# Token weights between the attention pairs, token products in thirds: the first batch of an attention and mixer kernel

## The chip, the cores and the metric

The kernel runs on one core of a Trainium2 chip. The metric is the device time of one execution in microseconds, as a median over runs. The core has five engines that run side by side and meet through semaphores: TensorE (PE in the profile; PEld is its weight load), VectorE (DVE), ScalarE (ACT), GpSimd (POOL) and SyncE (SP), which here issues nearly all DMAs. SBUF is the on-chip working memory, PSUM the eight banks into which matrix products go.

## The reference

There are 4 batches, 8 heads, 768 positions and head width 64. For each head, attention sees a band of 31 neighbours and 24 block summaries. A block is 32 positions: its key is the maximum over the block, its value the mean.

```
k_sum = k.reshape(B, H, nb, block, D).max(axis=3)
v_sum = v.reshape(B, H, nb, block, D).mean(axis=3)
scores_l = scale * q @ k^T          (kept where |i - j| < 16)
scores_s = scale * q @ k_sum^T + log(32)
a = softmax(concat(scores_l, scores_s));  x = a @ concat(v, v_sum)
```

The heads are laid side by side (x: 4 x 768 x 512), and a mixer follows: a token part that mixes positions through 256 columns, then a channel part through 1536 columns.

```
h = relu(x^T @ w_tok1) @ w_tok2;   u = x + h^T
out = u + relu(u @ w_ch1) @ w_ch2
```

## The kernel before, in words

**Stages.** The heads of a batch are taken in 4 pairs (`p`), each in two halves of the positions (`g`). For a pair, `key_blocks` reduces the block maxima (`ks`) and copies them behind the 96 window columns of each of the 12 key tiles (`k[:, :, 96:]`), PE makes the scores (`sc`), DVE adds the mask and finds the row minimum of the negated scores (`lowest`, one custom instruction for each of 128 x 120 scores, with a second one that reads out `den`), ACT takes the exponential (`power`), PE turns the result (`et`), ACT copies it out (`eT`), PE multiplies by the values (`av`), and DVE divides and writes `x` (`rec`, `x`). The channel part then runs one step behind: `ch1` makes `hp` from `u` and `w1`, ACT and DVE split it into high and low part `h`, and `ch2` adds to the four `acc` banks with `w2`. While it runs on one batch, the attention of the next is woven in. So only the first batch's attention stands alone: it fills the first part of the span.

**The first batch.** Its value means come from PE (`vm`, in `first_means`): 24 products for a pair, the two heads written to partitions 64 to 87 and 96 to 119 of one bank. Two DVE copies take them to `vs`, and two POOL copies spread them into the value tiles (`v`). `tok1` makes the first token product `t1p` of a pair: 12 products of 128 x 128 (each shows as two records in the trace), 6 position tiles times 2 column halves, bound to all three parts of `wt1`. ACT (`Relu`) and DVE split it into `t1`. `tok2` makes `up` from `x`, `t1` and both halves of the second token matrix, `wt2`, which it needs whole.

**Weights.** The weights are 64-bit words. `w_tick(i)` loads two jobs of 256 KB into a staging tile and turns them into 32-bit numbers: two ACT passes (`absolute` into `wt` or `wb`, `last_bits` into `wp`), one POOL pass (`clamp`), two DVE passes (`shift` into `wp`, `sign` into `wt` or `wb`). Ticks 0 to 2 fill the three parts of `wt1` directly. From tick 3 on there follow two ACT copies (high part) and two POOL subtractions (low part): ticks 3 to 5 are `wt2`, then each channel weight tile takes one tick. `WTAGS` says whose memory the staging tile of a tick borrows; a tick's load waits until that slot is free.

**What sets the order.** Each piece of work is an `add(engine, time, function, reads, writes, rank)`. `Plan` plays the list through with these times; of what is ready on an engine it takes the lowest rank, and among equals the earliest written. The order that comes out is then fixed: every engine works strictly in it, so a step whose input is late holds all behind it. The ranks are `R_H, R_EVAC, R_ATT, R_LATER, R_W, R_BACK`, lowest first. `bank(name, tags)` goes round the PSUM banks named in `tags`; `att` and `mm` have two banks each, `acc0` to `acc3` one. `APART` puts a pad of so many 32-bit words in front of the first tile of a tag in SBUF, so it shifts addresses and nothing else.

**Lines.** Numbers are of the kernel before: `key_blocks` L347 (maximum) and L356 (copy); `first_means` L376 (PE), L396 (DVE copies), L383 (POOL); `tok1` L752; `split_t1` L733 and L738; `tok2` L832, L840, L879, L884; `w_tick` L1473 and L1479 (ACT), L1486 (POOL), L1491 and L1498 (DVE), L1518 (ACT), L1524 (POOL); `lowest` L478, `power` L488; warm-up L1537. `between` on DVE, which the change calls, is one instruction with two tensor inputs:

```
nc.vector.scalar_tensor_tensor(
    out=out_, in0=left, scalar=1.0, in1=right, op0=ALU.mult, op1=op
)
```

Of the kernel before, what the change touches and what calls it, by code (L numbers as in the profile page):

```python
# [202 lines left out]
def tile_attention_mixer(  # L203
# [74 lines left out]
    def tok_bank(name, first=False):  # L278
        if state["phase"] == "start":
            return bank(name, ["acc0", "acc1"] if first else ["att", "att", "acc2"])  # L280
        return bank(name, BANKS[state["phase"]])
# [58 lines left out]
    def key_blocks(p):  # L340

        if p >= B * NP:
            return
        kt, ks = k_t[p], sbuf([P, NB], "ks", f"ks_{p}", 2)
        add(
            "dve", 0.98,
            lambda: nc.vector.tensor_reduce(  # L347
                out=ks.t.rearrange("p (t r) -> p t r", r=2),
                in_=kt.t[:, :, 16 : 16 + QT].rearrange("p t (r c) -> p t r c", c=32),
                axis=AX, op=ALU.max,  # L350
            ),
            reads=[(kt, 0)], writes=[(ks, 0)], rank=R_ATT,
        )
        add(
            "dve", 0.33,
            lambda: nc.vector.tensor_copy(  # L356
                kt.t[:, :, WIN:], ks.t.unsqueeze(1).broadcast_to([P, NT, NB])
            ),
            reads=[(ks, 0)], writes=[(kt, 1)], rank=R_ATT,
        )  # L360
# [4 lines left out]
    def first_means(p):  # L365

        pt, cs = vm_bank, slice(DTOK + D * p, DTOK + D * (p + 1))
        s = sbuf([P, 2 * D], "vs", f"vs_0_{p}", 2)
# [4 lines left out]
        def sums():  # L373
            for t in range(NT):
                for j in range(2):
                    nc.tensor.matmul(  # L376
                        pt.t[at[j] : at[j] + NB, cs],
                        lhsT=means[:, NB - 2 - 2 * t : 2 * NB - 2 - 2 * t],
# [3 lines left out]
        def spread(n, j):  # L382
            nc.gpsimd.tensor_copy(  # L383
                v_t[n].t[WIN:NC, :, :D],
                s.t[WIN:NC, j * D : (j + 1) * D].unsqueeze(1).broadcast_to([NB, NT, D]),
# [5 lines left out]
        )  # L391
        for j in range(2):
            n = 2 * p + j
            add(
                "dve", 0.15,
                lambda j=j: nc.vector.tensor_copy(  # L396
                    s.t[WIN:NC, j * D : (j + 1) * D], pt.t[at[j] : at[j] + NB, cs]
                ),
                reads=[(pt, p)], writes=[(s, j)], rank=R_EVAC,
            )  # L400
            add(
                "pool", 0.95, lambda n=n, j=j: spread(n, j), reads=[(s, j)],
                writes=[(v_t[n], 1)], rank=R_ATT,
            )
# [340 lines left out]
    def tok1(b, p):  # L745
# [3 lines left out]
        def products():  # L749
            for k in range(DTOK // P):  # L750
                for T in range(TT):
# [3 lines left out]
                        start=(T == 0), stop=(T == TT - 1),  # L755
                    )

        add(
            "pe", 2.8, products, reads=x_keys(b, p) + [(wt1, i) for i in range(3)],
            writes=[(pt, 0)], rank=R_ATT,  # L760
        )
# [629 lines left out]
    APART = {"u1": 32, "u0": 16, "ot": 32, "t1": 32, "w1": 16}  # L1391
# [32 lines left out]
    WTAGS = ["u0"] * 6 + ["k", "k", "q", "v", "x", "x"] * 4  # L1424
    assert 2 * len(WTAGS) == len(jobs)

    def w_tick(i, behind=()):
# [21 lines left out]
        first, rank = two[0][2] is None, R_ATT if i < 3 else R_LATER if i < 6 else R_W  # L1449
# [10 lines left out]
        else:  # L1460
            pb = bank(f"wp_{i}", ["acc3"] if i < 10 else ["att"])
# [45 lines left out]
        add("dve", 0.7, shift, reads=parts, writes=[(pb, 0)], rank=rank)  # L1507
        add("dve", 0.7 if room else 0.85, sign, reads=[*keys, (pb, 0)], writes=parts, rank=rank)
# [23 lines left out]
    add("dve", 0.3, lambda: nc.vector.memset(warm.t, 0.0), writes=[(warm, 0)])  # L1532
    pw = mm_bank("warm")

    def warm_up():
        for _ in range(17):
            nc.tensor.matmul(pw.t, lhsT=warm.t[:, :P], rhs=warm.t, start=True, stop=True)  # L1537

    add("pe", 5.2, warm_up, reads=[(warm, 0)], writes=[(pw, 0)])
# [170 lines left out]
```

## Time and profile before

| what | value |
|---|---|
| median of 3 runs | 562.3 us (561.27 to 563.73) |
| the profiled execution | 563.8 us, span 561.4 us |
| PE busy | 546.0 us, 97% of the span |
| PE weight loads | 484.5 us, 86% |
| DVE, ACT, POOL busy | 337.7, 267.9, 265.7 us |
| mean DMA rate | 179 GB/s |
| PE's share of the chain that ended last | 84% |

The span is the time between the first and the last instruction of the profiled execution; the execution's own time is 2.4 us longer. Busy times are sums over instructions, and PE's are modelled, because products overlap. The timeline lists instructions in order of time; the chain of waits goes back from the last instruction to whatever released each step; a waits row gives the total, the count and the longest wait. The start of the profile, up to the first `hp` at 63 us, is where nearly everything of the change lies.

### The profile page before, as it was taken

To read this page: it belongs to the slowest core of one execution; us is meant where nothing else is said; L and a number is where in the kernel's file an instruction comes from. 1 tells how busy PE (TensorE), PEld (TensorE's weight loads), DVE (VectorE), ACT (ScalarE), POOL (GpSimd) and SP (SyncE) were. 2 spreads that over 40 slices of the span, in tenths; PEclk is the share of its full clock that TensorE was granted. 3 is DMA by queue.
4 is the path that set the end of the run, shared out by engine and by line. 5 is a ranking of instruction groups with operands and counts; after the bars stand their busy time and mean duration, and the time that the engine had idled before them with its cause. 6 is when DMAs were issued, how large, how long until landed. Compare 5 with 4: busy or idle time off the path is not lost.

```text
span 561.4 us, 12755 instructions
## 1 busy us (share of the span) xinstructions
PE 546.0 (97%) x4625; PEld 484.5 (86%) x4625; DVE 337.7 (60%) x949; ACT 267.9 (48%) x771; POOL 265.7 (47%) x344
## 2 busy tenths in 40 slices
PE   7979999999989999999999999999999999999997
PEld 4769888878889988888799997888789999999997
DVE  4985668866553346455463436444352584898974
ACT  4776788853674334222252215332234342567642
POOL 2555478832134320168997420059879612454111
PEclk9979999999999999999999999999999999999999
DMA  8952569674655018759695506768788664543531
GB/s 330 396 177 76 188 196 281 184 234 140 193 171 164 19 43 213 207 175 255 200 279 147 110 18 187 168 173 232 184 239 260 175 231 133 179 139 109 177 103 63
DMA packets 134030, 100.30 MB, mean 179 GB/s; under 512 B 88272, under 2 KB 112464, under 8 KB 133968
## 3 DMA queue, kind: packets, MB, share of 16 engines
q1 hardware_dynamic: 133824, 99.31, 59.1%
q8 instruction: 36, 0.59, 0.4%
q14 instruction: 26, 0.21, 0.1%
q10 hardware_dynamic: 144, 0.20, 0.1%
HBM read 69.39 MB, written 28.31 MB: 174 GB/s over the span
## 4 chain that ended last, share of the span: by engine, by line
PE 84%; DMA 7%; DVE 4%; SPq 1%; ACT 1%; issue 1%; POOL 1%; ACTq 0%; DVEq 0%; POOLq 0%
PE hp L901 25%; PE acc L944 25%; PE up L840 6%; PE t1q L799 5%; PE av L598 3%; PE pb L1174 3%; PE sc L464 3%; PE t1p L752 2%; PE pa L1174 2%; PE qb L1174 2%; PE qc L1174 2%; PE pc L1174 2%; DMA vb<-in_vb 1%; DMA k<-in_kw 1%; PE et L528 1%; PE qa L1174 1%
## 5 line engine op out<-in xcount | busy, mean ns | idle before, releaser
L944 PE MATMUL acc<-h,w 128*128 128x512 f32 (+1 forms) x864 | 162.3, 337 | 0.0
L901 PE MATMUL hp<-u,w 128*128 128x512 f32 (+1 forms) x864 | 161.6, 336 | 0.0
L901 PEld LDWEIGHTS hp<-u,w 128*128 128x128 f32 x864 | 133.1, 188 | 18.2 <-issue 1.4
L944 PEld LDWEIGHTS acc<-h,w 128*128 128x128 f32 x864 | 132.0, 188 | 18.2 <-ACT h L913 1.4
L488 ACT ACTIVATE e<-e,den 128x120 f32<-128x120 f32 x192 | 69.8, 385 | 58.6 <-DVE den L478 52.7
L913 ACT ACTIVATE h<-hp 128x512 fp32r<-128x512 f32 (+1 forms) x72 | 35.2, 488 | 117.0 <-PE hp L901 116.6
L918 DVE SCALAR_TENSOR_TENSOR h<-hp,h 128x512 fp32r<-128x512 f32 (+1 forms) x72 | 39.7, 552 | 74.3 <-ACT h L913 74.1
L1021 POOL TENSOR_TENSOR s<-s,w 128x256 f32<-128x256 f32 x84 | 62.0, 744 | 5.1
L983 POOL TENSOR_TENSOR ot<-ot,u 128x512 f32<-128x512 f32 (+1 forms) x24 | 23.7, 1015 | 59.5 <-DVE ot L975 27.7
L478 DVE CUSTOM_DVE_ANT_0 e<-sc,mask_sb 128x120 f32<-128x120 f32 x192 | 41.3, 277 | 15.0 <-PE sc L464 12.3
L1524 POOL TENSOR_TENSOR w<-wb,w 128x256 fp32r<-128x256 f32 x48 | 34.6, 742 | 9.4 <-ACT w L1518 9.2
L840 PE MATMUL up<-wt,t 128*128 128x512 f32 (+2 forms) x192 | 39.0, 343 | 0.0
L447 POOL MEMSET e<- 128x48 f32 x16 | 2.2, 138 | 67.9 <-DMA away<-e 33.3
L785 POOL TENSOR_TENSOR xs<-x,xs 128x512 fp32r<-128x512 f32 x18 | 23.2, 1291 | 21.1 <-ACT xs L780 21.1
L840 PEld LDWEIGHTS up<-wt,t 128*128 128x128 f32 x192 | 30.4, 189 | 2.4
L420 DVE TENSOR_REDUCE vs<-vb 96x8 f32<-96x256 f32 (+1 forms) x40 | 18.4, 461 | 17.1 <-DMA vb<-in_vb 17.0
L464 PEld LDWEIGHTS sc<-k,q 64*64 64x64 f32 x768 | 19.9, 132 | 10.0 <-issue 9.2
L799 PE MATMUL t1q<-xs,ws 128*128 128x256 f32 x216 | 28.4, 283 | 0.0
L464 PE MATMUL sc<-k,q 64*64 64x120 f32 x768 | 26.8, 271 | 1.5 <-DVE k L356 1.5
L799 PEld LDWEIGHTS t1q<-xs,ws 128*128 128x128 f32 x216 | 27.0, 190 | 0.3
L488 ACT ACTIVATION_READ_ACCUMULATOR e<-e,den 128x1 f32 x144 | 27.1, 188 | 0.0
L598 PEld LDWEIGHTS av<-v,eT 120*64 120x64 f32 x768 | 23.8, 138 | 3.8 <-issue 2.4
(128 smaller groups left out, 870.5 us busy)
## 6 DMA issues: line engine op xcount, KB each, us to landing
w<-in_w_ch SPq DMA_DIRECT2D x48, 256.0 KB
k<-in_kw SPq DMA_DIRECT2D x16, 720.0 KB
v<-in_vw SPq DMA_DIRECT2D x24, 288.0 KB
q<-in_q SPq DMA_DIRECT2D x16, 384.0 KB
away<-e SPq DMA_DIRECT2D x16, 384.0 KB
eT<-away SPq DMA_DIRECT2D x64, 96.0 KB
sums<-s SPq DMA_DIRECT2D x24, 256.0 KB
w2d<-w SPq DMA_DIRECT2D x12, 512.0 KB
```

Of the source, the lines that this page charges most:

```text
L464: nc.tensor.matmul(tiles[j].t[c * QT : (c + 1) * QT, i * NC : (i + 1) * NC], lhsT=qt.t[rows, t * QT : (t + 1) * QT], rhs=kt.t[rows, t, :], ...
L478: nc.vector.tensor_tensor_reduce(out=e.t[:, j, i * P : i * P + NC], in0=tiles[j].t[:, i * NC : (i + 1) * NC], in1=mask_sb[:, mv, :], op0=A ...
L488: nc.scalar.activation(ei, ei, AF.Exp, bias=den_t[n].t[:, 1, T : T + 1], scale=-1.0, accum_out=den_t[n].t[:, 0, T : T + 1] if p >= NP else ...
L598: nc.tensor.matmul(pv[cs, T], lhsT=eT[:NC, T % (TT // 2), cs], rhs=v.t[:NC, 2 * T + c], start=True, stop=True,)
L799: nc.tensor.matmul(pt.t[:, 2 * P * k : 2 * P * (k + 1)], lhsT=ws[:, wp, T, ks], rhs=xs[:, xp, T], start=(c == 0 and k == 0 and T == 0 and ...
L840: nc.tensor.matmul(pt.t[:, :nt], lhsT=t1.t[:, part, ks], rhs=wt2[w].t[:, k, h0 : h0 + nt], start=(far and k == 0 and i == 0), stop=(k == D ...
L901: nc.tensor.matmul(pt.t[:, :nt], lhsT=w1_t[f].t[:, w, c], rhs=us[c].t[:, part], start=(i == 0), stop=(i == len(ops) - 1),)
L913: lambda: nc.scalar.activation(h.t[:, 0], pt.t[:, :nt], AF.Relu),
L918: lambda: nc.vector.scalar_tensor_tensor(out=h.t[:, 1], in0=pt.t[:, :nt], scalar=0.0, in1=h.t[:, 0].bitcast(F32), op0=ALU.max, op1=ALU.sub ...
L944: nc.tensor.matmul(slot.t[:, c0 : c0 + nt], lhsT=w2_t[f].t[:, w, o * P : (o + 1) * P], rhs=h.t[:, part], start=(f == 0 and w == 0 and part ...
L1021: nc.gpsimd.tensor_tensor(out=out_, in0=left, in1=right, op=op)
L1174: nc.tensor.matmul(bank_.t[:, :HS], lhsT=w(i), rhs=x(j), start=first and n == 0, stop=True, skip_group_check=True,)
```

## The change

- The six token ticks are no longer written behind all of the first batch's loads. The loads now go `v0 v1 k1 q1 v2 v3 k2 q2 w0 v4 v5 k3 q3 w1 v6 v7 w2 w3 w4 w5`, where `w` stands for a tick. Ticks 0 to 2 get rank `R_LATER` in place of `R_ATT`, so their steps give way to attention steps that are ready.
- The token product of a pair is three pieces of work, one for each part of `wt1`, with both column halves in each.
- The key maxima go behind the windows as `max(ks, ks)` in place of a copy.
- The first head's means fill 32 partitions in place of 24, so that one DVE copy of 56 partitions takes both heads; `vs` has half the columns.
- `up` of the first batch goes round five PSUM tags in place of three.
- The staging tiles of later ticks borrow in another order, ticks 6 to 9 go round two PSUM tags (`acc3`, `mm`) for `wp`, the pads change, three warm-up products go, and some planned times change.

```diff
-        return bank(name, ["acc0", "acc1"] if first else ["att", "att", "acc2"])
+        return bank(name, ["acc0", "acc1"] if first else ["att", "att", "acc2", "acc0", "acc1"])
...
+        def wide():
+            return ks.t.unsqueeze(1).broadcast_to([P, NT, NB])
...
-            "dve", 0.33,
-            lambda: nc.vector.tensor_copy(
-                kt.t[:, :, WIN:], ks.t.unsqueeze(1).broadcast_to([P, NT, NB])
-            ),
+            "dve", 0.37,
+            lambda: between("dve", kt.t[:, :, WIN:], wide(), wide(), ALU.max),
...
-                        pt.t[at[j] : at[j] + NB, cs],
-                        lhsT=means[:, NB - 2 - 2 * t : 2 * NB - 2 - 2 * t],
+                        pt.t[at[j] : at[j] + (32, NB)[j], cs],
+                        lhsT=means[:, NB - 2 - 2 * t : NB - 2 - 2 * t + (32, NB)[j]],
...
+            lambda: nc.vector.tensor_copy(s.t[at[0] : NC], pt.t[at[0] : NC, cs]),
...
-        def products():
-            for k in range(DTOK // P):
-                for T in range(TT):
+        def products(c):
+            for T in (2 * c, 2 * c + 1):
+                for k in range(DTOK // P):
...
+                        start=(T == 0 and k == 0), stop=(T == TT - 1), skip_group_check=True,
...
-        add(
-            "pe", 2.8, products, reads=x_keys(b, p) + [(wt1, i) for i in range(3)],
-            writes=[(pt, 0)], rank=R_ATT,
-        )
+        for c in range(TT // 2):
+            add(
+                "pe", 0.96, lambda c=c: products(c), reads=[*x_keys(b, p), (wt1, c)],
+                writes=[(pt, 0)], rank=R_ATT,
+            )
...
-    APART = {"u1": 32, "u0": 16, "ot": 32, "t1": 32, "w1": 16}
+    APART = {"u1": 32, "ot": 48, "t1": 16, "w1": 16}
...
-    WTAGS = ["u0"] * 6 + ["k", "k", "q", "v", "x", "x"] * 4
+    WTAGS = ["u0"] * 6 + ["k", "k", "q", "v"] + ["k", "k", "q", "v", "x", "x"] * 3 + ["k", "k"]
...
-        first, rank = two[0][2] is None, R_ATT if i < 3 else R_LATER if i < 6 else R_W
+        first, rank = two[0][2] is None, R_LATER if i < 3 else R_LATER if i < 6 else R_W
...
-            pb = bank(f"wp_{i}", ["acc3"] if i < 10 else ["att"])
+            pb = bank(f"wp_{i}", ["acc3", "mm"] if i < 10 else ["att"])
...
-        for _ in range(17):
+        for _ in range(14):
...
-    for p in range(NP):
-        if p:
-            load_k(p)
-            load_q(p)
-        load_v(2 * p)
-        load_v(2 * p + 1)
+    for what in 'v0 v1 k1 q1 v2 v3 k2 q2 w0 v4 v5 k3 q3 w1 v6 v7 w2 w3 w4 w5'.split():
+        {"k": load_k, "q": load_q, "v": load_v, "w": w_tick}[what[0]](int(what[1]))
...
-    for tick in range(6):
-        w_tick(tick)
```

On DVE, between the first and the second pair's scores (`ks_1`, `k_1` are the second pair's key maxima and keys, `vs` the means), before:

```order
L347 TENSOR_REDUCE ks_1_218<-k_1_113 128x24
L396 COPY vs_0_0_235<-vm_171 24x64 x2
L356 COPY k_1_113<-ks_1_218 128x12x24
L478 ISA e_1_0_279,den_2_280<-sc_2_0_246,mask_sb_71 128x120
L478 ISA den_2_280 128x1
```

and with the change:

```order
L351 TENSOR_REDUCE ks_1_214<-k_1_110 128x24
L396 COPY vs_0_0_231<-vm_167 56x64
L1024 SCALAR_TENSOR_TENSOR k_1_110<-ks_1_214 128x12x24
L478 ISA e_1_0_274,den_2_275<-sc_2_0_241,mask_sb_71 128x120
L478 ISA den_2_275 128x1
```

The sequence is the same; one mean copy stands where two stood, and the key copy is the two-input form.

On PE, at the end of the first batch's attention (heads 6 and 7 are the last pair; `t1p_0_0` is the first pair's token product), before:

```order
L598 MATMUL av_5_684<-v_5_408,eT_5_1_621 64x65 x6
L528 MATMUL et_6_0_706<-identf_66,e_3_0_583 120x128 x3
L528 MATMUL et_7_0_727<-identf_66,e_3_0_583 120x128 x3
L752 MATMUL t1p_0_0_744<-x_0_0_379,wt1_551 128x128 x12
L528 MATMUL et_6_1_771<-identf_66,e_3_1_654 120x128 x3
L528 MATMUL et_7_1_779<-identf_66,e_3_1_654 120x128 x3
L752 MATMUL t1p_0_1_785<-x_0_0_379,wt1_551 128x128 x12
L598 MATMUL av_6_817<-v_6_545,eT_6_0_722 64x65 x6
```

and with the change:

```order
L528 MATMUL et_6_0_703<-identf_66,e_3_0_593 120x128 x3
L752 MATMUL t1p_0_0_715<-x_0_0_374,wt1_378 128x128 x4
L528 MATMUL et_7_0_732<-identf_66,e_3_0_593 120x128 x3
L752 MATMUL t1p_0_0_715<-x_0_0_374,wt1_378 128x128 x4
L528 MATMUL et_6_1_748<-identf_66,e_3_1_656 120x128 x3
L528 MATMUL et_7_1_755<-identf_66,e_3_1_656 120x128 x3
L752 MATMUL t1p_0_1_761<-x_0_0_374,wt1_378 128x128 x4
L598 MATMUL av_6_771<-v_6_547,eT_6_0_730 64x65 x6
L598 MATMUL av_6_771<-v_6_547,eT_6_1_759 64x65 x6
L598 MATMUL av_7_788<-v_7_570,eT_7_0_745 64x65 x6
L598 MATMUL av_7_788<-v_7_570,eT_7_1_769 64x65 x6
L752 MATMUL t1p_0_0_715<-x_0_0_374,wt1_378 128x128 x4
```

The 12 products of the first pair stand in three places, two of them between the last pair's transposes and one behind its value products.

On DVE, around the second and third weight chunk (`w_1`, `w_2`; each has a `shift` into `wp` and a `sign` into `wt1`), before:

```order
L1498 SCALAR_TENSOR_TENSOR wt1_551<-w_1_356,wp_1_649 128x512
L396 COPY vs_0_3_682<-vm_171 24x64 x2
L1491 SCALAR_TENSOR_TENSOR wp_2_662<-wt1_551,wp_2_662 128x512
L606 TENSOR_SCALAR rec_4_710<-av_4_666 128x6
L609 RECIPROCAL rec_4_710<-rec_4_710 128x6
L618 TENSOR_TENSOR x_0_1_717<-av_4_666,rec_4_710 128x6x64
L606 TENSOR_SCALAR rec_5_724<-av_5_684 128x6
L609 RECIPROCAL rec_5_724<-rec_5_724 128x6
L618 TENSOR_TENSOR x_0_1_717<-av_5_684,rec_5_724 128x6x64
L1498 SCALAR_TENSOR_TENSOR wt1_551<-w_2_411,wp_2_662 128x512
L478 ISA e_3_1_654,den_6_584<-sc_6_1_605,mask_sb_71 128x120
L478 ISA den_6_584 128x1
```

and with the change:

```order
L396 COPY vs_0_3_679<-vm_167 56x64
L478 ISA e_3_1_656,den_7_617<-sc_7_1_602,mask_sb_71 128x120
L478 ISA den_7_617 128x1
L1499 SCALAR_TENSOR_TENSOR wt1_378<-w_1_281,wp_1_567 128x512
L606 TENSOR_SCALAR rec_4_711<-av_4_662 128x6
L609 RECIPROCAL rec_4_711<-rec_4_711 128x6
L618 TENSOR_TENSOR x_0_1_722<-av_4_662,rec_4_711 128x6x64
L606 TENSOR_SCALAR rec_5_727<-av_5_683 128x6
L609 RECIPROCAL rec_5_727<-rec_5_727 128x6
L618 TENSOR_TENSOR x_0_1_722<-av_5_683,rec_5_727 128x6x64
L1492 SCALAR_TENSOR_TENSOR wp_2_724<-wt1_378,wp_2_724 128x512
L1499 SCALAR_TENSOR_TENSOR wt1_378<-w_2_385,wp_2_724 128x512
```

The last pair's minima (`e_3_1`) now stand ahead of the second chunk's last step; four of them stood behind the third chunk's.

More of the change, by code (lines that the diff above doesn't have):

```diff
@@ L367, in first_means @@
         pt, cs = vm_bank, slice(DTOK + D * p, DTOK + D * (p + 1))
-        s = sbuf([P, 2 * D], "vs", f"vs_0_{p}", 2)
+        s = sbuf([P, D], "vs", f"vs_0_{p}", 2)
         at = (WIN - 32, WIN)
@@ L384, in spread @@
                 v_t[n].t[WIN:NC, :, :D],
-                s.t[WIN:NC, j * D : (j + 1) * D].unsqueeze(1).broadcast_to([NB, NT, D]),
+                s.t[at[j] : at[j] + NB].unsqueeze(1).broadcast_to([NB, NT, D]),
             )
@@ L391, in first_means @@
         )
+        add(
+            "dve", 0.23,
+            lambda: nc.vector.tensor_copy(s.t[at[0] : NC], pt.t[at[0] : NC, cs]),
+            reads=[(pt, p)], writes=[(s, 0)], rank=R_EVAC,
+        )
         for j in range(2):
@@ L394, in first_means @@
             add(
[L395 to L399, printed above, removed]
-            )
-            add(
-                "pool", 0.95, lambda n=n, j=j: spread(n, j), reads=[(s, j)],
+                "pool", 0.85, lambda n=n, j=j: spread(n, j), reads=[(s, 0)],
                 writes=[(v_t[n], 1)], rank=R_ATT,
@@ L754, in products @@
                         lhsT=wt1.t[:, T, k * P : (k + 1) * P], rhs=x2.t[:, T, a, :],
-                        start=(T == 0), stop=(T == TT - 1),
+                        start=(T == 0 and k == 0), stop=(T == TT - 1), skip_group_check=True,
                     )
-        add(
-            "pe", 2.8, products, reads=x_keys(b, p) + [(wt1, i) for i in range(3)],
-            writes=[(pt, 0)], rank=R_ATT,
-        )
+        for c in range(TT // 2):
+            add(
+                "pe", 0.96, lambda c=c: products(c), reads=[*x_keys(b, p), (wt1, c)],
+                writes=[(pt, 0)], rank=R_ATT,
+            )
         split_t1(
@@ L1506, in w_tick @@
         add("act", spent, last_bits, reads=keys, writes=[(pb, 0)], rank=rank)
-        add("dve", 0.7, shift, reads=parts, writes=[(pb, 0)], rank=rank)
-        add("dve", 0.7 if room else 0.85, sign, reads=[*keys, (pb, 0)], writes=parts, rank=rank)
+        add("dve", 1.0 if i < 6 else 0.7, shift, reads=parts, writes=[(pb, 0)], rank=rank)
+        add("dve", 1.0 if i < 6 else 0.7 if room else 0.85, sign, reads=[*keys, (pb, 0)], writes=parts, rank=rank)
         for j in range(0 if first else 2):
@@ L1531, in tile_attention_mixer @@
     warm = sbuf([P, 512], "vb", "warm", 1, F16)
-    add("dve", 0.3, lambda: nc.vector.memset(warm.t, 0.0), writes=[(warm, 0)])
+    add("dve", 1.0, lambda: nc.vector.memset(warm.t, 0.0), writes=[(warm, 0)])
     pw = mm_bank("warm")
     def warm_up():
-        for _ in range(17):
+        for _ in range(14):
             nc.tensor.matmul(pw.t, lhsT=warm.t[:, :P], rhs=warm.t, start=True, stop=True)
-    add("pe", 5.2, warm_up, reads=[(warm, 0)], writes=[(pw, 0)])
+    add("pe", 4.9, warm_up, reads=[(warm, 0)], writes=[(pw, 0)])
     load_k(0)
```

## The prediction

> **What bounds the kernel now.** I read the page first, then busy time and granted clock by windows, then PE's waits, the chain of waits and the timeline of the first 66 us. From the page, the span and PE's busy tenths in 40 slices; from the windows (length; busy PE, PEld, DVE, ACT, POOL; PEclk, DMA share, GB/s), the start, the stretch behind it and five short ones:
>
> ```profile
> span 561.4 us, 12755 instructions
> PE   7979999999989999999999999999999999999997
> 0.00:62.00 62.00, 53.56 (x786) 44.45 (x787) 43.09 (x166) 41.01 (x109) 29.65 (x52) 0.94 0.63 231
> 62.00:150.00 88.00, 88.00 (x612) 74.03 (x614) 61.70 (x164) 62.69 (x184) 48.40 (x69) 1.00 0.71 214
> 32.00:34.00 2.00, 1.06 (x8) 0.57 (x6) 1.91 (x4) 2.00 (x7) 1.13 (x2) 1.00 0.99 342
> 34.00:36.00 2.00, 0.00 (x0) 0.00 (x0) 1.83 (x7) 1.04 (x3) 1.54 (x2) 1.00 0.90 293
> 36.00:38.00 2.00, 1.01 (x4) 1.01 (x5) 2.00 (x11) 1.03 (x4) 0.00 (x0) 0.52 0.64 242
> 40.00:42.00 2.00, 2.00 (x11) 2.00 (x11) 1.68 (x2) 0.18 (x1) 0.86 (x2) 0.50 0.00 0
> 44.00:46.00 2.00, 2.00 (x19) 1.89 (x17) 0.42 (x1) 2.00 (x5) 1.10 (x2) 1.00 0.13 44
> ```
>
> From 62 us on PE is full at full clock, and what the start saves should reach the end. The start has 8.4 us without PE work (62.00 - 53.56), and these rows show the half clock there alone. What holds it there is in PE's waits (total, times, longest) and in the chain of waits (start, length, what):
>
> ```profile
> PE t1p L752 <- DVE den L478: 3.1, 1, 3.1
> PE sc L464 <- DVE k L356: 1.5, 1, 1.5
> PE up L832 <- DVE u L884: 0.5, 1, 0.5
> 36.99 5.49 PE t1p L752 x24
> 42.48 0.92 PE et L528 x6
> 43.40 2.68 PE t1p L752 x24
> 46.08 1.55 PE av L598 x48
> 47.63 5.55 PE t1p L752 x48
> 53.18 0.44 PE up L832 x4
> 63.06 2.78 PE hp L901 x12
> ```
>
> The first token product stands 3.1 us, then its 24 records take 5.49 us where the next 24 take 2.68: the pause cost the clock as well. The name "den" is only the last DVE row before it; what it really awaits is the third weight chunk, `wt` of L1498. The timeline of DVE, POOL and ACT shows it, with the copies that share its engines (start, length, row):
>
> ```profile
> 5.96 0.31 DVE L356 COPY k<-ks 128x288 f32<-128x288 f32 x1
> 12.04 0.48 DVE L396 COPY vs<-vm 24x64 f32<-24x64 f32 x2
> 12.40 0.83 POOL L383 COPY v<-vs 24x768 f32<-24x768 f32 x1 [2.19 <-DVE vs L396]
> 12.55 0.84 DVE L356 COPY k<-ks 128x288 f32<-128x288 f32 x1
> 17.91 0.76 DVE L356 COPY k<-ks 128x288 f32<-128x288 f32 x1
> 28.27 1.35 POOL L383 COPY v<-vs 24x768 f32<-24x768 f32 x1
> 28.97 1.20 DVE L1498 SCALAR_TENSOR_TENSOR wt<-w,wp 128x512 int32<-128x512 int32 x1
> 30.80 2.10 ACT L488 ACTIVATE e<-e,den 128x120 f32<-128x120 f32 x7
> 36.05 0.68 DVE L1498 SCALAR_TENSOR_TENSOR wt<-w,wp 128x512 int32<-128x512 int32 x1
> 44.29 0.42 DVE L738 SCALAR_TENSOR_TENSOR t<-t1p,t 128x256 fp32r<-128x256 f32 x1 [2.16 <-ACT t L733]
> 51.31 0.73 POOL L1524 TENSOR_TENSOR wt<-wb,wt 128x256 fp32r<-128x256 f32 x1 [0.27 <-ACT wt L1518]
> ```
>
> `wt` is complete at 36.05 + 0.68 = 36.73, and PE starts at 36.99.
>
> **Part by part: the token products.** A product of 24 records becomes three of 8, each bound to one weight chunk. In the new order PE runs the first third behind `et_6_0`, the second behind `et_7_0`, and only the last thirds need the third chunk. The pause is now filled with PE's own work, worth up to the 3.1 us, and the clock need not fall: 5.49 - 2.68 = 2.8 us. The instructions are as many as before.
>
> On the clock, the rows: PE has 1.06 us of work in 32 to 34 and none in 34 to 36, and the granted clock reads 0.52 from 36; it is full again only in the window from 44. [...]
>
> **The key maxima and the means.** The copy takes 0.31 us when POOL is idle, 0.84 and 0.76 when a POOL copy started just ahead of it: 12.40 + 0.83 = 13.23, and the key copy ends at 13.39. As a maximum it has two SBUF inputs. Its own time I work out from L738 and L1498: 0.42 us for 256 columns, 0.68 for 512, so 0.45 for 288; 0.14 us dearer than the free copy. The bounds are 0.31 and 0.84. That form does not escape POOL either: L1498 takes 1.20 us at 28.97, where POOL's copy runs to 29.62. [...]
>
> But the order turns. The two mean copies (0.48) become one of 0.24, so the maximum starts at about 12.30, ahead of POOL's 12.40, and ends at 12.75 instead of 13.39: 0.64 us earlier, and POOL waits instead. The same at 17.91 gives 0.6 more. Together DVE is 1.2 us ahead when it leaves the second key block, and PE's 1.5 us wait shrinks by 0.64. The first maximum costs its 0.14, covered by the idle DVE ahead of the second keys' arrival; the three warm-up products taken off PE (0.2 us each once warm) go the same way. The fourth key maximum and those of later batches pay 0.14 us each on a DVE that is not the bound there.
>
> **The weights between the pairs.** Two loads of 256 KB now stand ahead of the third pair's values and the fourth pair's keys, two more ahead of its values. The queue's rate in 40 slices of 1.75 us:
>
> ```profile
> GB/s 0 306 368 302 409 406 412 421 404 419 419 389 399 383 392 376 220 155 303 280 335 143 0 0 59 91 0 0 9 162 281 6 0 242 62 215 241 243 219 280
> w<-in_w_tok SPq DMA_DIRECT2D x12, 256.0 KB
> k<-in_kw SPq DMA_DIRECT2D x4, 720.0 KB
> 11.05 0.95 DVE L347 TENSOR_REDUCE ks<-k 128x24 f32<-128x768 f32 x1 [0.64 <-DMA k<-in_kw]
> ```
>
> At about 390 GB/s each chunk delays what follows by 1.35 us. Summing the slices, the fourth keys (7.2 MB in line) have moved by 20.4 us; the second keys (2.8 MB, moved by 9.8) were seen at 11.05, so I add 1.3: 21.7. DVE comes to them at about 22, behind the first chunk's shift: covered, barely. A later arrival is paid one for one. The first chunk lands near 17.9, and ACT, where its two passes stand ahead of `eT_2_0`, idles some 0.4 us for it.
>
> Then DVE from the fourth key maximum (ends about 23.6, against 23.4 now, with a weight shift already done) to the second chunk's end. It has 18 masked minima at 0.20, two heads' scalings at 0.9, two mean copies and three weight steps of 0.69, and I add 0.5 twice for a POOL copy in the way, as at 28.97:
>
> ```profile
> 14.59 0.28 DVE L478 CUSTOM_DVE_ANT_0 e<-sc,mask_sb 128x120 f32<-128x120 f32 x1
> 14.79 0.28 DVE L478 CUSTOM_DVE_ANT_0 e<-sc,mask_sb 128x120 f32<-128x120 f32 x1
> 34.27 0.16 DVE L606 TENSOR_SCALAR rec<-av 128x6 f32<-128x6 f32 x1
> 35.16 0.15 DVE L606 TENSOR_SCALAR rec<-av 128x6 f32<-128x6 f32 x1
> ```
>
> (Minima start 0.20 apart, scalings 0.89.) That is 3.6 + 1.8 + 0.5 + 2.1 + 1.0 = 9.0: the second chunk at about 33, third at 36.5, as today. ACT, full from 22 on, gives the last pair's exponentials (12 at 0.30, from the row at 30.80) by about 33.3; today six of them wait behind weights until past 38. So PE has `et_6_0` near 32, the first third to 33.2, `et_7_0`, the second third to about 34.6. From 32.3 PE has four token products (4 x 2.68), three transposes (1.3) and two value products (1.55), 13.6 us, to 45.9. I add 1.0 for ACT's queue, where two weight passes stand between `eT_7_0` and `eT_7_1`: 46.9.
>
> **What is late next.** `up` needs the second token matrix. Its last low part ends today at 52.04, 1.1 us ahead of `up`, so it becomes the bound as soon as PE gains more than that. In the new order the passes for it on ACT, DVE and POOL are interleaved with the products' own evacuations; walked with the rows above they end between 47.0 and 47.7. I take `up` at 47.5 against 53.18: 5.7 us. Two more PSUM banks for `up` take the 0.5 us wait away: 6.2. Each hand-over between engines costs 0.1 to 0.2 us that my walk mostly leaves out; I give 0.9 back for those in a row here. **Sum: -5.3 us**, of which the half clock is 2.8 and the pause and smaller waits 2.5. The channel weights behind it lose no cover: `w_10` and `w_11` take key slots instead of waiting for `x`.
>
> The profiled execution took 563.8 us, 2.4 around its span and 1.5 above the median of 562.3. Its span would become 556.1, its time 558.5; the median becomes **557.0**. Half a per cent is 2.8 us, about what a measurement can tell: faster means below 559.5.
>
> **Rivals.** *Half clock stays* (0.15): PE pauses again, now inside the thirds, and the clock drops as before. For: the second third waits for a DVE step behind all minima, and `et_6_1`, `et_7_1` stand behind it. Against: the second chunk (8.1 MB in line, 24.0 us by the same sum) lands 9 us before its third is due. The 2.8 us stay lost: 559.8, the same.
>
> *The second token matrix decides* (0.10): its low part comes not before 50 us since ACT is full. For: the margin of 1.1 us today. Against: its loads start earlier. `up` gains 3.2 and its bank wait 0.5: 558.6, faster.
>
> *All hand-overs hide* (0.08): no reserve, and DVE gets its 0.5 twice back: -7.2, 555.1.
>
> *New addresses slow the products* (0.05): the APART table and the earlier weight tiles move `u0`, `e` and `t1` in SBUF. Groups of 12 products do not all take the same time:
>
> ```profile
> 100.38 2.72 PE hp L901 x12
> 120.19 2.95 PE acc L944 x12
> ```
>
> The slow ones stand behind attention work here, which speaks against addresses; nothing in the trace excludes them. If all 72 groups of 512 columns took 2.95, that is +16.6 us: 573.6, slower. It decides from about 35 groups on, where the loss passes 5.3 + 2.8.
>
> *The change does nothing* (0.02): a chunk arrives too late for its third: 562.3.
>
> **The numbers.** The forecast has 0.60, with its own range of 554.8 to 559.2 (the reserve gone; two more blocked copies and a late key block). Faster: 0.60 + 0.10 + 0.08 = 0.78; same: 0.15 + 0.02 = 0.17; slower 0.05. The range of 554.0 to 560.5 leaves out the last two rivals and the edges.
>
> **What would show it.** Right: the granted clock stays 1.00 in 36 to 44; no PE wait above 1.5 us between 25 us and `up`; `up` begins near 47.5 and `hp` near 57; key maxima take 0.4 to 0.5 us, the second ending before 13; from 62 us on PE stays full. Wrong: `t1p` records at half clock, PE waiting for `wt` or `x`, `up` waiting for POOL's low part, a DVE wait for keys near 22, or `hp` and `acc` groups above 2.72 where no attention work stands ahead of them.

## The result and the profile after

The changed kernel takes 555.04 us (median of 4 runs, 554.91 to 556.05), the kernel before 562.46 (median of 4, 561.27 to 563.73): a ratio of 0.9872 with a 95% interval of 0.9847 to 0.9896. The forecast was 557.0 with a range of 554.0 to 560.5. The profiled execution took 554.91 us, against 563.8 before.

From the page of the changed kernel: the span, PE's busy tenths in 40 slices and the granted clock.

```profile
span 553.1 us, 12744 instructions
...
PE   7999999999999999999999999989999999999997
...
PEclk9999999999999999999999999999999999999999
```

The third slice, 7 before, is 9 now (90% or more), and the dip in the clock is gone. The windows (length; busy PE, PEld, DVE, ACT, POOL; PEclk, DMA share, GB/s) show the start up to the first `hp`, and the places where the old kernel stood still and then ran at half clock:

```profile
0.00:56.00 56.00, 50.94 (x791) 42.46 (x792) 42.44 (x163) 41.83 (x109) 29.44 (x51) 1.00 0.71 255
...
32.00:34.00 2.00, 1.32 (x11) 1.12 (x11) 1.93 (x5) 2.00 (x7) 1.77 (x2) 1.00 0.92 322
34.00:36.00 2.00, 1.82 (x17) 1.85 (x18) 1.90 (x6) 1.60 (x4) 0.61 (x1) 1.00 0.81 256
36.00:38.00 2.00, 2.00 (x43) 1.88 (x42) 1.97 (x3) 2.00 (x5) 0.61 (x1) 1.00 0.29 109
```

The start has 5.1 us without PE work (56.00 - 50.94) where it had 8.4, and PE works 3.14 of the 4 us from 32 to 36 where it worked 1.06. PE's waits (total, times, longest) and the chain of waits (start, length, what) for the same stretch:

```profile
PE av L598 <- DMA eT<-away: 1.4, 1, 1.4
...
PE sc L464 <- DVE k L1024: 0.9, 1, 0.9
```

```profile
34.69 0.89 PE t1p L752 x8
...
38.68 8.26 PE t1p L752 x72
46.94 0.44 PE up L833 x4
...
56.12 2.76 PE hp L902 x12
```

The 3.1 us wait of `t1p` and the wait of `up` for `u` are gone; the wait for the second keys went from 1.5 to 0.9. `hp` begins at 56.12 where it began at 63.06: 6.94 us earlier. The largest wait left lies at 370 us, in a later batch's attention, and was 0.2 before.

The timeline of the changed kernel, DVE, POOL and PE, at the key maxima and at the first third:

```profile
12.36 0.46 DVE L1024 SCALAR_TENSOR_TENSOR k<-ks 128x288 f32<-128x288 f32 x1
12.47 1.04 POOL L385 COPY v<-vs 24x768 f32<-24x768 f32 x1 [2.22 <-DVE vs L396]
...
31.67 0.28 DVE L478 CUSTOM_DVE_ANT_0 e<-sc,mask_sb 128x120 f32<-128x120 f32 x1
31.88 1.26 DVE L1499 SCALAR_TENSOR_TENSOR wt<-w,wp 128x512 int32<-128x512 int32 x1
...
32.26 1.06 PE L752 MATMUL t1p<-x,wt 128*128 128x128 f32 x8
34.18 0.52 PE L528 MATMUL et<-identf,e 128*120 128x128 f32 x3 [0.86 <-DVE rec L606]
```

The maximum starts before POOL's copy and takes 0.46 us; POOL takes 1.04 instead of 0.83. The last minimum of the fourth pair (31.67) now stands ahead of the second weight chunk (31.88 to 33.14), and the first third starts at 32.26.

### The profile page after: what moved, and what is told of

Its sections match the earlier page's. It is cut to its first block, busy times and chain, and to the rows that moved or that the text cites. A ratio compares the mean times of both kernels' runs of the same rounds, so it can differ in the third digit from the quotient of the medians.

```text
span 553.1 us, 12744 instructions
## 1 busy us (share of the span) xinstructions
PE 541.3 (98%) x4622; PEld 481.2 (87%) x4622; DVE 337.7 (61%) x945; ACT 267.8 (48%) x771; POOL 265.7 (48%) x344
## 4 chain that ended last, share of the span: by engine, by line
PE 85%; DMA 9%; DVE 3%; SPq 1%; issue 1%; ACT 0%; ACTq 0%; DVEq 0%
PE hp L902 26%; PE acc L945 26%; PE up L841 6%; PE t1q L800 5%; PE av L598 3%; PE pb L1175 3%; PE sc L464 3%; PE pa L1175 2%; PE qb L1175 2%; PE qc L1175 2%; PE pc L1175 2%; DMA q<-in_q 2%; PE t1p L752 2%; DMA w<-in_w_tok 1%; PE qa L1175 1%; DMA w<-in_w_ch 1%
## 5 line engine op out<-in xcount | busy, mean ns | idle before, releaser
L598 PE MATMUL av<-v,eT 120*64 120x64 f32 (+1 forms) x768 | 26.3, 224 | 1.9 <-DMA eT<-away 1.4
```

What stands on the lines that cost most here:

```text
L598: nc.tensor.matmul(pv[cs, T], lhsT=eT[:NC, T % (TT // 2), cs], rhs=v.t[:NC, 2 * T + c], start=True, stop=True,)
```

## The experiments

All ratios are to the kernel before on the same chip; its medians there were 562.37 us (beside e1, e2, e3, e8), 563.36 (e4 to e7) and 561.93 (e9 to e12, on another chip, so these compare with the rest by their ratios). Two marks from the timelines split start from rest: the first `up`, and the first `acc`, which stands behind all of the first batch's `up` in every order. (The timeline has a group up to 0.3 us earlier than the chain.)

| kernel | ratio (95%) | median us | first up | first acc |
|---|---|---|---|---|
| before | 1 | 562.46 | 53.02 | 70.30 |
| changed | 0.9872 (0.9847 to 0.9896) | 555.04 | 46.78 | 63.33 |
| e1: changed, whole token product | 0.9900 (0.9865 to 0.9934) | 556.21 | 49.70 | 66.25 |
| e2: before, thirds alone | 1.0042 (1.0019 to 1.0066) | 564.65 | 53.23 | 70.66 |
| e3: before, filler in t1p's bank | 1.0058 (1.0037 to 1.0078) | 565.76 | 54.68 | 71.93 |
| e4: changed, plain key copy | 0.9857 (0.9834 to 0.9879) | 554.87 | 46.99 | 63.53 |
| e5: changed, two mean copies | 0.9856 (0.9831 to 0.9881) | 554.37 | 46.44 | 63.69 |
| e6: changed, old pads | 0.9923 (0.9895 to 0.9951) | 558.42 | 47.16 | 63.71 |
| e7: changed, old banks for up | 0.9881 (0.9854 to 0.9907) | 556.43 | 47.19 | 64.60 |
| e8: before, new loads and ranks | 1.0016 (0.9996 to 1.0036) | 562.71 | 49.26 | 66.67 |
| e9: e8 with the new pads | 0.9961 (0.9945 to 0.9977) | 560.13 | 50.22 | 67.62 |
| e10: before, filler in a free bank | one run | 558.50 (before 561.93) | 50.14 | 67.39 |
| e11: before, t1p in a free bank | one run | 558.47 (before 561.93) | 48.69 | 65.95 |
| e12: changed, e4's and e5's edits | 0.9905 (0.9890 to 0.9920) | 556.78 | 46.86 | 65.36 |

**e1_whole and e2_thirds: the thirds with and without the rest.** The changed kernel with `tok1` of before, and the other way round (e1's edit, in part):

```diff
-            for T in (2 * c, 2 * c + 1):
-                for k in range(DTOK // P):
+            for k in range(DTOK // P):
+                for T in range(TT):
...
-        for c in range(TT // 2):
-            add(
-                "pe", 0.96, lambda c=c: products(c), reads=[*x_keys(b, p), (wt1, c)],
-                writes=[(pt, 0)], rank=R_ATT,
-            )
+        add(
+            "pe", 2.8, products, reads=x_keys(b, p) + [(wt1, i) for i in range(3)],
+            writes=[(pt, 0)], rank=R_ATT,
+        )
```

> The changed kernel with the token product of a pair in one piece again; the loads, ranks, maxima, banks and pads stay. The plan now puts the first whole product behind the last pair's value products. Theory (the order of DVE and ACT steps is what fills PE, the thirds only close a small gap): the third chunk is done near 36.5 us, PE stands at most 1.5 us at a time, the granted clock stays 1.00, up begins near 48 instead of 46.94, and the time is 555.5 to 557. Rival (the thirds fill the pause): PE stands about 3 us again, the clock falls to half, up begins at 51 or later and the time is 559 to 562.

> The kernel before with the token product in thirds and nothing else. Theory: the first third runs near 34 us, but the second stands behind a transpose that needs minima which DVE makes only after the third chunk's last step at 36.7; PE stands over 3 us there, the clock falls to half all the same, up begins at 52 to 53.5 and the time is 561 to 563. Rival (the thirds fill the pause by themselves): no PE wait above 1.5 us, clock 1.00, up near 48 to 50, time 557 to 559.

In e1 PE's timeline has a pause of 2.1 us, and the windows (PE alone; then PEclk, DMA share, GB/s) the half clock behind it:

```profile
34.49 1.34 PE L528 MATMUL et<-identf,e 128*120 128x128 f32 x9 [2.12 <-DVE rec L606]
35.76 2.99 PE L598 MATMUL av<-v,eT 120*64 120x65 f32 x48
```

```profile
32.00:34.00 2.00, 0.37 (x3) 1.00 0.87 277
34.00:36.00 2.00, 1.51 (x13) 0.93 0.90 294
36.00:38.00 2.00, 2.00 (x39) 0.50 0.39 141
```

So the expected time came, but not by the expected way: the clock did fall, the value products took 2.99 us (1.62 in the changed kernel), and the start is 2.9 us later (66.25 against 63.33). It does not fall each time: in two of e1's five runs the mean clock over the span is 1.000. The whole lost less, 1.2 by the medians, with intervals that overlap: PE's gaps behind 66 us (those over 0.12 us, added up from the timeline) sum to 1.0 us in e1 and to 3.0 in the changed kernel, 2.0 of the 2.9.

In e2 there is no gain; the median is 2.3 us above that of before, and the interval excludes 1. (Its profiled execution also stood at half clock from 13.9 to 17.3 us, which before did not, and reaches the pause 1.3 us later.) PE, then DVE, from its timeline:

```profile
34.61 0.54 PE L528 MATMUL et<-identf,e 128*120 128x128 f32 x3 [1.03 <-ACT eT L539]
38.23 2.08 PE L752 MATMUL t1p<-x,wt 128*128 128x128 f32 x8 [3.08 <-DVE den L478]
...
37.30 0.68 DVE L1499 SCALAR_TENSOR_TENSOR wt<-w,wp 128x512 int32<-128x512 int32 x1
37.90 0.28 DVE L478 CUSTOM_DVE_ANT_0 e<-sc,mask_sb 128x120 f32<-128x120 f32 x1
```

These 8 records are the first third, which needs only the first chunk, ready long before (at 31.40). It starts at 38.23, behind the minimum that ends at 38.18, and not behind the chunk (37.98). What it waits for must be something that the minimum releases.

**e3_fill: 14 products on zeros in the pause.** The pause was to be filled, to see whether the clock holds:

```diff
+        def fill():
+            for _ in range(14):
+                nc.tensor.matmul(pt.t, lhsT=warm.t[:, :P], rhs=warm.t, start=True, stop=True)
...
+            add(
+                "pe", 0.01, fill, reads=x_keys(b, 1) + [(warm, 0)], writes=[(pt, 0)],
+                rank=R_H, behind=state["last_turn"],
+            )
```

> The kernel before with 14 products of zeros (512 columns, nothing of them is used) put on PE between the two transposes and the first token product, where PE stands 3.1 us; every other instruction keeps its place. Theory (of the 3.1 us pause and the 5.49 us product, 2.8 us are the clock): the clock stays 1.00 in 36 to 44 and the first token product takes about 2.7 instead of 5.49 us; up begins 2.0 to 2.8 us earlier, since the second token matrix's passes follow the products' evacuations; time 559.5 to 560.5. Rival (the second token matrix is the bound at 52.04): up gains at most 1.1 us, time 561.3 or more.

```profile
36.86 4.87 PE L762 MATMUL t1p<-warm 128*128 128x512 f16 x14 [3.08 <-DVE den L478]
41.56 2.84 PE L754 MATMUL t1p<-x,wt 128*128 128x128 f32 x24
```

The filler missed the pause: it needs no weight chunk, and the `x` of the second pair that it reads was done at 26.90, but it stood still all the same, until 36.86, and then paid for the half clock in the product's place. What it has in common with the product is the bank that it writes, `acc0`. In the kernel before, what lay there last is `sc_6_1`, the scores of head 6 in the fourth pair's second half. DVE takes three minima from it, and the third stands right behind the third weight chunk's last step (the last rows of DVE's order before, above). Its row in the timeline of before:

```profile
36.65 0.28 DVE L478 CUSTOM_DVE_ANT_0 e<-sc,mask_sb 128x120 f32<-128x120 f32 x1
```

It ends at 36.93, and the product starts at 36.99.

**e11_bank: the first token product in another bank.** The chunk and the bank can be told apart:

```diff
-        pt = tok_bank(f"t1p_{b}_{p}", True)
+        pt = plan.slot(ps, [P, 512], F32, "acc2", "t1p_0_0", 1) if p == 0 and state["phase"] == "start" else tok_bank(f"t1p_{b}_{p}", True)
...
-            for k in range(DTOK // P):
-                for T in range(TT):
+            for T in range(TT):
+                for k in range(DTOK // P):
```

> The kernel before, with the first token product in the bank of the means instead of the score bank, and its products in the order of the weight chunks; the planner's order stays on PE. Theory (in the kernel before the product waits for its bank, whose last minimum stands on DVE behind the third weight chunk, so thirds alone could not start earlier): 16 of its 24 records run near 33.9 to 35.7, the last 8 near 37, PE's wait there is 1.0 to 1.6 instead of 3.1, and the product ends at 37.7 to 38.5 instead of 42.3. Rival (it waits for a weight chunk alone): the wait stays at 2.8 to 3.1 and all records stand behind it.

```profile
33.80 1.95 PE L752 MATMUL t1p<-x,wt 128*128 128x128 f32 x16
36.89 1.16 PE L752 MATMUL t1p<-x,wt 128*128 128x128 f32 x8 [1.14 <-DVE wt L1498]
```

The bank decides. With the products in the order of the chunks, as in e2, but in a bank that is free, 16 records run at once, and only the last 8 wait for the third chunk, 1.14 us. The granted clock stays at 1.00, the first `acc` comes 4.35 us earlier, and the one run takes 558.47 us, 3.5 below the median of before. (The free bank with the old order of the products was not tried.)

**e10_fill2: the filler again, in a free bank.** As e3, with `ft = plan.slot(ps, [P, 512], F32, "acc2", "fill", 1)` written in place of `pt`, and without the `x` among the filler's reads.

> The kernel before, with 14 products on zeros put between the transposes of head 6's and 7's first half and the first token product, now into the bank of the means, which is free then; nothing else moves. Theory (the pause alone takes the clock down): the fillers run from 33.9 to 36.9, the granted clock stays at 1.00 to 46, the first token product takes 2.7 instead of 5.5 us and ends near 39.7; up still waits for the second token matrix, so it starts no earlier than 51.5 and the whole gains 0.5 to 1.7 us. Rival (the clock falls for another reason, such as the load of the other engines or the products themselves): the windows from 36 to 42 show 0.5 again with the pause filled.

```profile
33.68 3.19 PE L765 MATMUL fill<-warm 128*128 128x512 f16 x14
36.92 2.94 PE L754 MATMUL t1p<-x,wt 128*128 128x128 f32 x24
39.70 0.82 PE L528 MATMUL et<-identf,e 128*120 128x128 f32 x6
```

The token product starts where it did (36.92 against 36.99) and takes 2.78 us to the next row, where it took 5.28 (36.99 to 42.27): 2.5 us. The first `acc` is 2.9 earlier. With the pause filled the clock stays at 1.00, so in this one run, against a profiled execution of before that stood at half clock for 6.8 us, the clock is worth 2.5 to 2.9 us by itself. One part of the expectation failed: `up` was to wait for the second token matrix until 51.5, and began at 50.14. The matrix's passes move up with the products between which they are queued.

**e8_loads, e6_pads and e9_loads_pads: loads, ranks and addresses.** e8 is the kernel before with the list of loads and the rank of ticks 0 to 2 as changed, nothing else.

```diff
-        first, rank = two[0][2] is None, R_ATT if i < 3 else R_LATER if i < 6 else R_W
+        first, rank = two[0][2] is None, R_LATER if i < 3 else R_LATER if i < 6 else R_W
...
+    for what in 'v0 v1 k1 q1 v2 v3 k2 q2 w0 v4 v5 k3 q3 w1 v6 v7 w2 w3 w4 w5'.split():
```

> The kernel before with the new order of loads and the lower rank of the token ticks and nothing else: two mean copies, plain key copies, whole token products, old banks and pads. Theory (the order gives most, the rest needs the mean copies and the thirds): the minima of the last pair stand ahead of the third chunk, that chunk is done near 37, PE stands 2 to 3 us for it; up begins at 49 to 50 if the clock holds (time 557.5 to 559), at 52 if it falls (time 560 to 561.5). Rival (the loads alone are the gain): up at 47.5 or before, time 554.5 to 556.

The first `acc` is 3.63 us earlier, the clock is full from 32 to 46, and still the time is that of before. (Its profiled execution took 568.72 us, 6.0 above the kernel's median; of it only the start and the groups are used.) The groups by form, x432 each, with total busy time and mean ns, for e8:

```profile
L944 PE MATMUL acc<-h,w 128*128 128x512 f32 x432 | 107.5, 397 | 0.7 <-ACT h L913 0.7
L901 PE MATMUL hp<-u,w 128*128 128x512 f32 x432 | 107.1, 397 | 0.0
L901 PE MATMUL hp<-u,w 128*128 128x256 f32 x432 | 57.7, 283 | 0.0
```

and the same groups of the changed kernel:

```profile
L945 PE MATMUL acc<-h,w 128*128 128x512 f32 x432 | 105.8, 394 | 0.0
L902 PE MATMUL hp<-u,w 128*128 128x512 f32 x432 | 104.8, 392 | 0.0
L902 PE MATMUL hp<-u,w 128*128 128x256 f32 x432 | 56.2, 279 | 0.0
```

In these forms PE needs 5.5 us more; against before, over all four forms, it is 3.9 (327.8 to 323.9). Some 1.2 us of that is not the products' own: in this execution the clock fell once more, from 383.1 to 386.5 us, behind a wait of 1.9 us in a later batch's attention, and five `hp` products there took 2.33 us together, where 0.23 each is usual (2.77 for 12). The other 2.7 us are most of the 3.6 that the start gained. PE's gaps behind 66 us sum to 7.1 us here, against 3.3 in before; how much of that the other runs of e8 have is not known. Memory is handed out in the order of the work, so the new order of loads lays `u0`, `e` and `u1` elsewhere: with the old pads `u0` goes from byte 181632 to 162752 and `u1` from 172352 to 188800, with the new ones to 162688 and 188736 (the addresses are those of the built kernels). Before and in the changed kernel `u0` starts on a multiple of 128 bytes and `u1` halfway between two; in e8 it is the other way round. e6 tests that on the changed kernel, with the order of every engine kept (its expectation has it that `u0`, `e` and `t1` lie where they lay before; in the built kernel `u0`, `e` and `u1` lie where e8 has them):

```diff
-    APART = {"u1": 32, "ot": 48, "t1": 16, "w1": 16}
+    APART = {"u1": 32, "u0": 16, "ot": 32, "t1": 32, "w1": 16}
```

> The changed kernel with the old table of pads, so that u0, e and t1 lie where they lay before the change; the order of every engine stays. Theory (addresses cost and bring nothing here): first hp at 56.1 +- 0.2, the last groups of 12 products of 256 columns 1.36 us apart, the time 554.5 to 555.8. Rival (addresses set the rate of the products, so the last stretch's 1.41 returns): 0.05 more in each of the groups it touches, 1 to 4 us: 556.0 to 559.0.

e6's time is 558.42 us, 3.6 and 4.1 above e4 and e5 on the same chip. From its timeline, two neighbouring groups, and then at the same place in the changed kernel:

```profile
82.99 2.93 PE L902 MATMUL hp<-u,w 128*128 128x512 f32 x12
85.75 2.93 PE L945 MATMUL acc<-h,w 128*128 128x512 f32 x12
```

```profile
82.36 2.88 PE L902 MATMUL hp<-u,w 128*128 128x512 f32 x12
85.08 2.88 PE L945 MATMUL acc<-h,w 128*128 128x512 f32 x12
```

A group starts 2.77 us after the last one, against 2.72, and over the four forms PE is busy 326.2 us against 322.6, with the clock at 1.00 in both: 3.6 us, which is the loss. The rival held. In the other direction, e9 gives e8 the new pads:

> The kernel before with the new order of loads and ranks, as in the earlier run with these alone, and the new table of pads with it; the order of every engine is that of the earlier run. Theory (the new order of loads lays u0 and its neighbours elsewhere in SBUF, and without the new pads the products of u and w run at 2.77 and 1.42 us per group of 12 instead of 2.72 and 1.37, 72 groups x 0.05 = 3.6 us, which eats the start's gain): groups back at 2.72 and 1.37, hp rows of 256 columns at 56.2 to 56.6 us in all instead of 57.7, and 558.5 to 560.0 where the earlier run had 562.7. Rival (the gain goes in later waits for eT and u, whatever the addresses): 561.5 to 563.0.

```profile
L944 PE MATMUL acc<-h,w 128*128 128x512 f32 x432 | 106.8, 395 | 0.7 <-ACT h L913 0.7
L901 PE MATMUL hp<-u,w 128*128 128x512 f32 x432 | 105.0, 392 | 0.0
L901 PE MATMUL hp<-u,w 128*128 128x256 f32 x432 | 56.2, 279 | 0.0
```

The products of `u` are back, and the ratio goes from 1.0016 to 0.9961, intervals apart: 3.1 us. The time, 560.13, is a touch above what was expected. The clock fell in this profile (below), but that doesn't account for it: the two of the six runs with a mean clock of 1.000 took 560.08 and 560.85 us.

**e4_copy, e5_means and e12_plain: the key maxima and the means.** e4 puts the plain copy back (the edit below), e5 the two mean copies, e12 both.

```diff
-            lambda: between("dve", kt.t[:, :, WIN:], wide(), wide(), ALU.max),
+            lambda: nc.vector.tensor_copy(kt.t[:, :, WIN:], ks.t.unsqueeze(1).broadcast_to([P, NT, NB])),
```

> The changed kernel, with the key blocks spread by the plain copy again instead of a maximum; the order of every engine stays. Theory (what counts is that DVE starts ahead of POOL, which one mean copy instead of two brings about, not the form of the instruction): the copy still starts near 12.36 us, some 0.1 ahead of POOL's, takes 0.31 to 0.5 instead of 0.46, PE's wait for the second keys stays at 0.8 to 1.0, and the time is 554.5 to 556.0. Rival (the maximum holds POOL off where a copy does not): copies that meet POOL take 0.75 to 0.85 again, the wait grows to 1.2 to 1.5, the fourth keys are 0.6 to 1.0 later, and the time is 555.5 to 556.5.

> The changed kernel, with two mean copies on DVE and two means in two parts of the tile again, as before the change; the planner's order moves by some rows with it. Theory (the single copy turns the order of DVE and POOL): POOL's copy starts ahead again, the second maximum takes 1.0 to 1.3 us and ends at 13.4 to 13.7, PE's wait for the second keys is 1.4 to 1.8 instead of 0.9, up starts 0.5 to 1.5 later than 46.94, and the time is 555.5 to 557.0. Rival (DVE has slack in the start, and PE's token products set up): up starts within 0.3 of 46.94 and the time is 554.5 to 555.5.

In e4 the copy still comes first and is free of POOL:

```profile
11.97 0.31 DVE L356 COPY k<-ks 128x288 f32<-128x288 f32 x1
12.08 0.89 POOL L383 COPY v<-vs 24x768 f32<-24x768 f32 x1 [2.20 <-DVE vs L394]
```

in e5 POOL comes first and holds the maximum up:

```profile
12.70 0.83 POOL L385 COPY v<-vs 24x768 f32<-24x768 f32 x1 [2.26 <-DVE vs L398]
12.86 0.97 DVE L1026 SCALAR_TENSOR_TENSOR k<-ks 128x288 f32<-128x288 f32 x1
```

So the order decides, as the theory of e4 and the first half of e5's said, and the form of the instruction does not. In before, the changed kernel, e4 and e5 the one that starts second takes longer: the maximum 0.97 us (e5) against 0.46 when it is first (changed), the plain copy 0.84 (before) against 0.31 (e4), and POOL's copy 0.89 behind the copy (e4) and 1.04 behind the maximum (changed) against 0.83 (before and e5). But the end of e5 is e5's rival: PE waits 1.7 us for the second keys, and `up` begins 0.3 us earlier than in the changed kernel, not later (the first `acc` 0.4 later), and the time is the same. What is lost at 12 us is not there any more at 46: the changed kernel's two gaps at 26 us, 0.73 together, and that of 0.86 at 33.3 are missing in e5. Neither edit alone brings anything that shows.

> The changed kernel without its edits to the key blocks and the means: the plain copy and two mean copies again, the rest (loads, ranks, thirds, pads, banks) as changed. Theory (those two edits buy nothing, since DVE has slack until the token products): the wait for the second keys is 1.4 to 1.7, up starts at 46.3 to 47.3, and the time is 554.0 to 555.5, the ratio within 0.003 of the changed kernel's. Rival (each alone is covered by the other, both undone are not): up 0.6 to 1.2 later than 46.94, 555.7 to 557.

Both undone cost 1.9 us by the ratios (0.9905 against 0.9872; the intervals touch, but e12's lies apart from those of e4 and e5), and not by either expected way: `up` starts on time (46.86), and then waits for `u`, at 54.4 and 56.2:

```profile
PE up L833 <- DVE u L885: 1.5, 2, 0.8
```

The planner's order of DVE moves with the edits there; which row of it does that was not tried.

**e7_banks: the banks for up.**

```diff
-            return bank(name, ["acc0", "acc1"] if first else ["att", "att", "acc2", "acc0", "acc1"])
+            return bank(name, ["acc0", "acc1"] if first else ["att", "att", "acc2"])
```

> The changed kernel with the old three banks for up in the first batch. Theory (the two banks take away only the wait for u): up starts at 46.9 +- 0.3, PE waits some 0.5 to 0.7 for it, first hp at 56.5 to 56.9, the time 555.3 to 556.0. Rival (the channel weights' banks and the order behind it lean on it too): more than one new wait behind up, first hp at 57 or later, the time 556.2 or more.

```profile
PE up L833 <- DVE u L885: 0.6, 1, 0.6
```

The wait for `u` is back with its 0.6 us, alone, as the theory said; but the first `hp` at 58.2 and the median of 556.43 are those of the rival. The first `acc` is 1.3 later (0.4 of it before `up`). The interval overlaps that of the changed kernel, and this profile has a fall of the clock at 374.8 us besides, so what the banks are worth in all isn't clear of the noise; in the start it is about 1 us.

No version beats the changed kernel: e4 and e5 stand at 0.9857 and 0.9856 with intervals around its 0.9872.

## Why the prediction was right, and where it was not

**The half clock, -2.8.** Right in cause, and in size for the profiled execution. The clock stays at 1.00, and e10, which fills the pause and changes nothing else, measures 2.5 to 2.9. That it would hold with shorter pauses was the author's estimate, which no row of before shows: it held in the changed kernel, where PE waits 0.86 us inside the thirds, and it fell in e9, with no gap above 0.91 us from 32 us on (last section). The price was read from an execution that lost two stretches of 3.41 us to the half clock (below); where before loses less, the gain is smaller.

**The pause.** Right in what goes, wrong in why. The prediction said: "what it really awaits is the third weight chunk". The chunk was ready at 36.73 and the bank at 36.93, and PE started at 36.99; the profile's own name, `den`, was the true one. That the time predicted came all the same is luck: the change also frees the bank, which the prediction did not ask of it. The reading turns the parts round: thirds bound to chunks cannot start while the bank is taken (e2, no gain), and a free bank with the products in the chunks' order brings 4.35 of the 6.97 us that the start gains (e11, one run). In the changed kernel it is the new order of loads and the lower rank of the ticks, not tried apart, that free the bank, since the fourth pair's minima now stand ahead of the second and third chunk on DVE; the thirds then keep PE busy behind it (e1, 2.9 us in the start).

**The walk through the start.** The terms hit: maximum 0.46 us (0.45), its end 12.82 (12.75), the fourth at 23.17 + 0.46 = 23.63 (23.6), the second chunk at 33.14 (33), the third at 36.52 (36.5), the first third begun at 32.26. One missed: the second third ended at 35.6 and not at 34.6, since `et_7_0` waited 0.86 us for the bank of `av_4`, which `x` frees at 34.03 (the row names `rec`, which stands right behind that `x`; in the built kernel `et_7_0` and `av_4` have one bank). It didn't matter, for `up` begins at 46.94 against 47.5: the matrix's last low parts (four subtractions on POOL from 43.15 on, 3.33 us) end at 46.48, where the prediction had 47.0 to 47.7. So PE's products, by half a microsecond, and not the matrix set `up`, and the rival of the second token matrix falls, in e10 too (its matrix ends at 49.26, and `up` begins at 50.14).

**The reserve, +0.9.** The term that was mis-sized. The walk to 47.5 was the matrix's, and it ended at 46.48 with its hand-overs in it (most of those in the start of before take 0.03 to 0.16 us, where 0.1 to 0.2 was the author's estimate); so the reserve had nothing to pay for, and the start gained 6.94 us, against 5.3 with the reserve and 6.2 without. The number of the rival with all hand-overs hidden, 555.1, came out, with a chance of 0.08, but by luck: it wanted DVE's half microsecond back twice, and the second chunk's two steps took 1.08 and 1.26 us on DVE where 0.69 each was the price without POOL. The forecast's own range, 554.8 to 559.2, holds 555.04 too, but the reserve gone gives only 556.1; its lower end was not worked out.

**The key maxima and the means.** Priced rightly, and neither needed alone (that POOL would be the one to wait was an estimate; its copy took 1.04 us behind the maximum, against 0.83): their 0.64 us at PE's wait is real (1.5 to 0.9) and does not reach `up` (e4, e5, e12). With both undone the time is lost behind `up`, as DVE's order moves.

**Behind the start.** "From 62 us on PE is full" holds only nearly: PE's gaps behind 66 us sum to 3.3 us before and 3.0 after, and go from 1.0 to 3.9 over the changed kernel and its variants (e1 and e4 to e7). They are waits of later attention for its data, they differ with each order, and they can decide whether a start gain of 2.9 us shows as 2.9 or as 1.2 (one profile of each kernel). The start's 6.97 us, 0.3 from the gaps and 1.3 from the channel products (323.9 to 322.6) make 8.6, where the profiled span is 8.3 shorter; the medians differ by 7.4, since the profiled execution of before was 1.3 us above its median.

**The rival of the addresses.** Its sign was the wrong way round. The change to the pads isn't a risk of the change but a condition of it: without it the products take 3.6 us more in the changed kernel (e6), the new pads bring the loads and ranks 3.1 us (e9), and without the pads these alone bring nothing (e8). The price, 0.05 us for a group, was not in the rows that the prediction took for it (2.72 and 2.95).

Open are the wait at 370 us (1.4 in the changed kernel, 0.4 in e1) and which tile's address it is that slows the products: `u0`, `e` and `u1` moved together, and the `acc` products of 512 columns, whose own tiles `h` and `w2` did not move, slowed in e6 as well (106.6 against 105.8).

## What to carry to other kernels

When the last releaser and your reading of the wait are two tenths of a microsecond apart, find what each of them frees, the bank too, since that decides which edit works alone. Whenever the order of allocations changes, compare the time of one and the same product group before and after: here a shift of `u0`, `e` and `u1` by 64 bytes was worth 3.1 us (e8 against e9), where the order won 3.6 in the start. And fill a pause that costs the clock with products that have no wait of their own: 14 on zeros were worth 2.5 to 2.9 us of the start here, in one run.

## What the runs showed of the hardware

The clock fell without a pause of 3 us, too: in e9 the longest gap from 32 to 36 us is 0.91, and it fell to 0.50. Within each trace, the clock changes only at steps of 3.41 us (before: full for 9 steps, half for 2, full again for 152), and where the steps lie differs from run to run. PE's work is read here in the step just ahead of the change. For before, and then for e9 (PE alone; then PEclk, DMA share, GB/s):

```profile
32.66:36.07 3.41, 0.54 (x3) 1.00 0.95 315
36.07:42.90 6.83, 5.91 (x27) 0.50 0.19 71
```

```profile
33.01:36.42 3.41, 1.81 (x13) 1.00 0.87 291
36.42:39.84 3.42, 3.42 (x18) 0.50 0.35 126
```

Over all 14 traces, leaving out the last 3 us of each, the clock fell behind 8 steps, in which PE worked 0.54 to 1.93 of the 3.41 us (1.30 in e1), and it held behind every step with more than 1.93; 8 steps with 1.68 to 1.93 held as well, so PE's busy time alone does not draw the line exactly. The emptiest steps around 32 to 39 us had 2.50 (e8), 2.32 (e11) and 2.55 us (changed) and held. It is also not the same in each run: e9's mean clock over the span is 1.000 in two of its six runs and 0.995 to 0.998 in the others. And it has a price over whole runs: of the 48 runs of before beside the experiments, the 20 with a mean clock of 0.996 or 0.997 have a median of 561.9 us, the 28 with 0.992 to 0.994 one of 563.1.

In e1 and e9 PE was at work for 38 and 53% of the step ahead of the fall (1.30 and 1.81 of 3.41 us), and the clock fell all the same. In e9's step three gaps of 0.91, 0.35 and 0.34 us make 1.60 us together.
